# Attention and expert MLP in one kernel: GpSimd instead of VectorE chooses the experts of the side slots, and the last batch's ranks stand two product groups later

## The chip, the cores and the metric

The kernel runs on one core of a Trainium2 chip. The metric is the device time of one execution in microseconds (us). The kernel before has a median of 1017.33 us over 3 runs (1016.41 to 1018.0).

## What is computed

Attention over 8 batches of 8 heads, 576 tokens each, with a threshold under the maximum of each row, followed by a layer that sends each of the 4608 tokens to one of 8 experts:

```python
scores = scale * np.matmul(q, k.transpose(0, 1, 3, 2))          # (8, 8, 576, 576), head_dim 64
thresh = np.max(scores, axis=-1, keepdims=True) - tau
scores = np.where(scores >= thresh, scores, -1000000000.0)
attn = softmax(scores);  x = (attn @ v) as (4608, 512)
logits = x @ w_gate + modality_bias[modality_id]                # (4608, 8)
e_idx = np.argmax(logits, axis=1)
for e in range(8):
    mask = e_idx == e
    h = np.maximum(x[mask] @ w1[e], 0.0)                        # 512 -> 1024
    out[mask] = gate_w[mask, None] * (h @ w2[e])                # 1024 -> 512
```

## The kernel before

**Attention.** A batch has four pairs of heads and a pair has nine steps, so the attention runs over 288 steps. In a step TensorE forms 128 rows of scores against all 576 keys for one head (L427, tile `s` from `km` and `q`), VectorE takes the row maximum (L460), a short VectorE operation adds the threshold (L467), ScalarE exponentiates (L470), VectorE masks and sums (L484, tile `pr`), and TensorE transposes and multiplies by the values (L512, L546). A step's scores cannot be overwritten before L484 of an earlier step has read them, so TensorE waits at L427 when VectorE is late. The keys and queries of the next pair are split into a high and a low part on GpSimd (L338 and L339: `nk`, `qb`, `nq`), and SyncE copies the parts into place (L379 `km`, L373 `q`).

**Routing.** When a batch is through, `route_a`, `route_c` and `route_b` compute logits, the one-hot choice `oh` (L692) and the rank of every token within its expert: six small matmuls of `oh` against a triangle `ltri` and against ones (their line is that of the helper, L546), then `pos` (L709), the running count, and `posi`. Five indirect DMAs on GpSimd (L719, tile `tab`) scatter the token numbers into a table in DRAM.

**Side slots.** The expert MLP of 256 to 512 tokens at a time is woven into the attention of later batches: seven side slots, one for each batch from the second on, and the rest in last slots behind the attention. For each side slot `pick(w)` (lines 728 to 743) finds an expert that has at least `w` tokens left in the table: eight VectorE operations on rows of eight values, whose results are the expert's number and its first row, tile `pk_i`. It is issued 14 steps ahead of the slot. SyncE loads the two numbers into registers (L832, L836), reads the row of token numbers from the table (L838, tile `tb`), and loads weights (L878, L882). GpSimd gathers the tokens with indirect DMAs (L854, `xg`), TensorE transposes them (L868), GpSimd splits the weights (L898, L900), and TensorE multiplies (L914 for the first layer, L941 for the second; VectorE writes `hl` at L926 between them). `done` holds how many units of 64 rows of each expert are given away, and `pick_rest` (L745 to L808) plans the last slots from it: about 40 VectorE operations that end in the table `si` (L795), with which SyncE loads the first last slot.

**What sets the order.** TensorE and GpSimd run in the order in which the program is written out: a dictionary `C` gives a time in steps to every piece, and pieces are emitted by that time. In each of the product loops of a slot a group is three matmuls of 128x512 (high times high, low times high, high times low). The other engines are ordered by a scheduler. The entry `'end'` of `C` places the pieces of the last batch; its last number is the place of `route_b`, in steps behind the start of the last pair.

Of the kernel before, what the change touches and what calls it, by code (L numbers as in the profile page):

```python
# [11 lines left out]
F32 = mybir.dt.float32  # L12
# [5 lines left out]
ALU = mybir.AluOpType  # L18
AX = mybir.AxisListType
# [10 lines left out]
def tile_attn_moe(  # L30
# [16 lines left out]
         'wL': [-5.5, -4, -2.5, 2.7, 12, 13.3, 14.6, 21, 3.8, 4.9, 6, 7.1, 15.8, 22.2, 23.4, 24.6], 'ask': 4, 'gat0': [-8.4, -8.3], 'xt0': [-2, -1], 'rows0': -9.6, 'gat1': [-9.6, -9.5, -5], 'fill': (8, 8.5), 'fpool': (3,), 'route0': (18, 18, 20), 'gap': (1.0, 0.75), 'exp': -12.5, 'two': 98, 'end': (12, 13, (15, 16), (13.5, 13.6, 14.1, 14.2), 14.5, 15, 16.5), 'xf': 9, 'early': [], 'parts': ((((7, 0, 2), (9, 2, 5)), ((11, 0, 2), (13, 2, 5))), (((6, 0, 2), (8, 2, 4), (10, 4, 5)), ((12, 0, 2), (14, 2, 5)))), 'xp': ((15, 16), (16, 17)), 'prepp': ((0, 1, 2), (0, 0, 2)), 'trp': ((7, 11), (6, 12))}  # L47
    nc = tc.nc
    B, H, S, D = q.shape
    NE = wg.shape[1]  # L50
# [12 lines left out]
    W = 512  # L63
    NCH = -(-N // W)
    LAP = 640
    TS = 8
# [7 lines left out]
    U = 64  # L74
# [15 lines left out]
    tiny = ctx.enter_context(tc.tile_pool(name="tiny", bufs=2))  # L90
    wp = ctx.enter_context(tc.tile_pool(name="wp", bufs=1))
    xp = ctx.enter_context(tc.tile_pool(name="xp", bufs=1))
# [44 lines left out]
    def load_first():  # L137
# [3 lines left out]
        for s in range(2):  # L141
            for z, src in enumerate((k, q)):
# [3 lines left out]
                if s == 0:  # L146
# [17 lines left out]
                            base=0, pattern=[[1, P]], channel_multiplier=-1)  # L164
# [16 lines left out]
    iota_1 = iota([1, NE], [[1, NE]], "iota_1", base=1)  # L181
# [10 lines left out]
    for t in oh2:  # L192
# [5 lines left out]
    taken0 = iota([1, NE], [[LAP * TS + 1, NE]], "taken0", base=W * TS)  # L198
    nc.gpsimd.tensor_scalar(out=taken0, in0=taken0, scalar1=1.0 / (U * TS), scalar2=None, op0=ALU.mult)
# [5 lines left out]
                            base=0, pattern=[[1, NE], [-1, NE]], channel_multiplier=0)  # L205
    cnt = glob.tile([1, 4, NE], F32, name="cnt")
# [27 lines left out]
    done = glob.tile([1, NE], F32, name="done")  # L234
# [493 lines left out]
    def pick(w):  # L728

        a = tiny.tile([1, NE], F32, name="pk_a", bufs=1)  # L730
        nc.vector.scalar_tensor_tensor(out=a, in0=done, scalar=float(-U * TS), in1=base[0][0:1, :],
                                       op0=ALU.mult, op1=ALU.add)
        nc.vector.scalar_tensor_tensor(out=a, in0=a, scalar=float(w * TS), in1=iota_1, op0=ALU.is_ge, op1=ALU.mult)
        r = tiny.tile([1, 1], F32, name="pk_r", bufs=1)
        nc.vector.tensor_reduce(out=r, in_=a, axis=AX.X, op=ALU.max)
        nc.vector.tensor_scalar(out=a, in0=iota_1, scalar1=r, scalar2=None, op0=ALU.is_equal)
        t2 = tiny.tile([1, NE], F32, name="pk_d", bufs=1)
        nc.vector.scalar_tensor_tensor(out=t2, in0=a, scalar=float(U * TS), in1=done, op0=ALU.mult, op1=ALU.mult)
        si = tiny.tile([1, 2], I32, name="pk_i")
        nc.vector.tensor_reduce(out=si[:, 1:2], in_=t2, axis=AX.X, op=ALU.max)  # L740
        nc.vector.tensor_scalar(out=si[:, 0:1], in0=r, scalar1=-1.0, scalar2=0.0, op0=ALU.add, op1=ALU.max)
        nc.vector.scalar_tensor_tensor(out=done, in0=a, scalar=float(w // U), in1=done, op0=ALU.mult, op1=ALU.add)
        return si[:, 0:1], si[:, 1:2]

    def pick_rest():  # L745
# [3 lines left out]
        nc.vector.scalar_tensor_tensor(out=left, in0=done, scalar=float(-U * TS), in1=base[0][0:1, :],  # L749
                                       op0=ALU.mult, op1=ALU.add)  # L750
# [4 lines left out]
        for z, w in enumerate((WM, WH, 0)):  # L755
# [9 lines left out]
                                       scalar=float(U) / W, in1=cnt[:, 0:3, :], op0=ALU.mult, op1=ALU.add)  # L765
# [521 lines left out]
```

## Time and profile before

| What | Value |
|---|---|
| median of 3 runs | 1017.33 us (1016.41 to 1018.0) |
| the profiled execution | 1013.78 us |
| its span (first to last instruction) | 1012.0 us, 1.8 us less than its own time |
| mean granted TensorE clock | 0.997 of full speed |
| TensorE matmuls, busy | 988.0 us, 98% of the span |
| VectorE busy | 682.5 us, 67% |
| ScalarE busy | 636.1 us, 63% |
| GpSimd busy | 528.0 us, 52% |
| chain that ended last | TensorE 85%, VectorE 7%, issue 3%, GpSimd 2%, ScalarE 2%, DMA 1% |

The profiled execution is 3.55 us below the median of the runs; differences are worked out within it and then set against the median. The chain is followed back from the last instruction through what released each step; an engine that is not in the chain at some point may be changed there without effect, as long as it does not come into it.

### The profile page before, as it was taken

What the parts mean: (1) busy time and instruction counts of PE and PEld (TensorE: products, weight loads), DVE (VectorE), ACT (ScalarE), POOL (GpSimd) and SP (SyncE); (2) the same over time, 40 slices, a digit from 0 to 9 for tenths busy, and PEclk for the clock granted to TensorE, in tenths of its full rate; (3) what the DMA queues carried; (4) which work ended last, traced back from release to release, by engine and by line L of the source; (5) the groups of instructions that cost most, each with busy time, mean ns of one, the idle gap of its engine ahead of it and who ended that gap; (6) DMA issues with size and microseconds to landing.
All of it is one profiled execution on the core that took longest, in us unless ns stands there. A gap on an engine that the chain in (4) does not pass through costs nothing.

```text
span 1012.0 us, 20320 instructions
## 1 busy us (share of the span) xinstructions
PE 988.0 (98%) x6556; PEld 796.1 (79%) x6556; DVE 682.5 (67%) x1696; ACT 636.1 (63%) x1448; POOL 528.0 (52%) x733
## 2 busy tenths in 40 slices
PE   7999999999998999999999999999999999999997
PEld 6777678788887887888778887788878868888885
DVE  6888977787677776777677777777676765333422
ACT  5787887776666666666667666666666635334430
POOL 4354466386537554645546554646567374634311
PEclk9999999999999999999999999999999999999999
DMA  6667577677646765586645655567665336734301
GB/s 153 158 148 177 140 188 186 171 184 201 170 126 158 194 159 147 124 202 158 183 110 140 168 158 151 144 154 200 165 155 148 88 92 178 224 101 145 105 20 44
DMA packets 207139, 152.22 MB, mean 150 GB/s; under 512 B 100110, under 2 KB 168078, under 8 KB 207024
## 3 DMA queue, kind: packets, MB, share of 16 engines
q1 hardware_dynamic: 199776, 131.74, 51.2%
q0 software_dynamic: 7248, 19.09, 6.1%
q8 instruction: 54, 0.88, 0.4%
q14 instruction: 61, 0.50, 0.2%
HBM read 80.05 MB, written 19.87 MB: 99 GB/s over the span
## 4 chain that ended last, share of the span: by engine, by line
PE 85%; DVE 7%; issue 3%; POOL 2%; ACT 2%; DMA 1%; POOLq 0%; DVEq 0%; ACTq 0%; SPq 0%
PE bk L546 15%; PE s L427 15%; PE bk L512 11%; PE bk L941 10%; PE bk L914 10%; PE pm L941 8%; PE pm L914 8%; PE bk L364 2%; DVE pr L484 2%; DVE nm L460 2%; PE bk L868 2%; PE bk L537 2%; PE bk L598 1%; ACT e L470 1%; PE bk L645 1%
## 5 line engine op out<-in xcount | busy, mean ns | idle before, releaser
L460 DVE TENSOR_REDUCE nm<-s 128x1 f32<-128x576 f32 x254 | 190.9, 752 | 101.0 <-PE s L427 99.6
L484 DVE SCALAR_TENSOR_TENSOR pr<-s,nm,e 128x576 f32<-128x576 f32 x254 | 204.7, 815 | 61.6 <-ACT e L470 58.9
L470 ACT ACTIVATE e<-s,nm 128x576 f32<-128x576 f32 x254 | 188.8, 744 | 62.5 <-DVE nm L460 56.6
L427 PE MATMUL s<-km,q 128*128 128x288 f32 x1024 | 197.2, 314 | 9.9 <-DVE pr L484 8.1
L522 ACT COPY ptm<-bk 128x512 f32<-128x512 f32 x256 | 149.4, 584 | 54.0 <-PE bk L512 53.2
L512 PE MATMUL bk<-ident,pr 128*128 128x128 f32 x1152 | 174.7, 274 | 0.0
L427 PEld LDWEIGHTS s<-km,q 128*128 128x128 f32 x1024 | 146.9, 189 | 26.9 <-DVE pr L484 19.7
L512 PEld LDWEIGHTS bk<-ident,pr 128*128 128x128 f32 x1152 | 141.3, 141 | 27.2 <-issue 6.2
L546 PE MATMUL bk<-ptm,v_m 128*64 128x320 f32 (+1 forms) x1024 | 140.7, 412 | 0.0
L900 POOL TENSOR_TENSOR w2l<-raw,w2h 128x512 fp32r<-128x512 f32 x77 | 98.4, 1287 | 32.6 <-ACT w2h L896 28.5
L546 PEld LDWEIGHTS bk<-ptm,v_m 128*64 128x64 f32 x1024 | 68.2, 136 | 50.6 <-issue 8.6
L956 POOL DMA_INDIRECT out_dram<-y,tb x37 | 37.6, 1017 | 122.1 <-DVE y L954 92.6
L501 ACT COPY rp<-pr 128x64 f32<-128x64 f32 x271 | 60.1, 248 | 42.5 <-DVE pr L484 40.2
L338 POOL CAST nk<-str 128x64 fp32r<-128x64 f32 x31 | 7.4, 239 | 144.1 <-ACT str L352 138.7
L914 PE MATMUL bk<-xh,w1h 128*128 128x512 f32 (+3 forms) x204 | 82.2, 403 | 0.1
L914 PE MATMUL bk<-xl,w1h 128*128 128x512 f32 (+3 forms) x204 | 74.1, 363 | 0.0
L914 PE MATMUL bk<-xh,w1l 128*128 128x512 f32 (+3 forms) x204 | 74.1, 363 | 0.0
L941 PE MATMUL bk<-w2h,hh 128*128 128x512 f32 x168 | 73.3, 436 | 0.0
L900 POOL TENSOR_TENSOR w1l<-raw,w1h 128x512 fp32r<-128x512 f32 x53 | 68.2, 1287 | 4.2
L941 PE MATMUL bk<-w2h,hl 128*128 128x512 f32 x168 | 66.3, 394 | 0.0
L941 PE MATMUL bk<-w2l,hh 128*128 128x512 f32 x168 | 66.0, 393 | 0.0
L900 DVE TENSOR_TENSOR w1l<-raw,w1h 128x512 fp32r<-128x512 f32 x27 | 19.3, 720 | 59.4 <-ACT w1h L896 59.4
(217 smaller groups left out, 1999.0 us busy)
## 6 DMA issues: line engine op xcount, KB each, us to landing
raw<-in_moe_w_dram SPq DMA_DIRECT2D x160, 256.0 KB, 3.6
q<-nq SPq DMA_DIRECT2D x124, 256.0 KB, 4.8
km<-nk SPq DMA_DIRECT2D x124, 144.0 KB, 2.5
v_m<-in_v_dram SPq DMA_DIRECT2D x32, 256.0 KB, 4.1
xs<-xr SPq DMA_DIRECT2D x32, 256.0 KB, 2.5
k_m<-in_k_dram SPq DMA_DIRECT2D x62, 128.0 KB, 3.0
q_m<-in_q_dram SPq DMA_DIRECT2D x62, 128.0 KB, 3.7
vr<-in_v_dram SPq DMA_DIRECT2D x64, 16.0 KB, 3.6
```

The lines of the kernel that those rows point to most:

```text
L427: nc.tensor.matmul(out=sps[:, hf, 0:SH], lhsT=a, rhs=x, start=(z == 0), stop=(z == len(passes) - 1))
L460: in_line(nc.vector.tensor_reduce(out=nm[:, 0:1], in_=sv, axis=AX.XY, op=ALU.max, negate=True), two)
L470: in_line(nc.scalar.activation(out=e, in_=sv, func=AF.Exp, bias=nm[:, 0:1]), two and n < LEAD)
L484: in_line(nc.vector.scalar_tensor_tensor(out=pr.rearrange("p (a x) -> p a x", a=2), in0=s2[n % 2][:, :, 0:SH], scalar=th, in1=e, op0=ALU.i ...
L501: (nc.gpsimd.tensor_copy if 2 <= n < 46 else nc.scalar.copy)(out=state[("rp", p)][:, 2 * c + s + x, :], in_=pr[:, SA:S])
L512: nc.tensor.transpose(out=ps[:, kc * P:(kc + 1) * P], in_=pr[:, kc * P:(kc + 1) * P], identity=ident)
L522: in_line(nc.scalar.copy(out=ptm[:, s, :, (c % 2) * P:(c % 2 + 1) * P], in_=pv), n + 2 < LEAD)
L546: nc.tensor.matmul(out=o, lhsT=lhsT, rhs=rhs, start=start, stop=stop, skip_group_check=True)
L900: then(eng.tensor_tensor(out=lo, in0=raw, in1=hi.bitcast(F32), op=ALU.subtract), eng is nc.vector and (lined or late))
L914: nc.tensor.matmul(out=ps[:, 0:WT], lhsT=a[:, cs], rhs=x[:, c, :], start=(c == 0 and z == 0), stop=(c == KC - 1 and z == 2))
L941: nc.tensor.matmul(out=ps, lhsT=h[:, ts], rhs=w, start=(z == 0 and y == 0), stop=(z == F2 - 1 and y == 2))
L956: i = _inst(nc.gpsimd.indirect_dma_start(out=out, out_offset=bass.IndirectOffsetOnAxis(ap=tb[:, t, 0:1].bitcast(U32), axis=0), in_=y, in_o ...
```

## The change

It has two parts. First, `pick` runs on GpSimd: 16 operations in place of 8, because each of the two reductions over eight values becomes four `tensor_scalar` operations on a single element, each of which folds in two more values as scalars that are read from memory (`fold`; the last of the four folds in one). `done` is now kept in the table's units, so one scaling operation at the start goes and `pick_rest` subtracts directly. Second, `'end'` has 17.5 in place of 16.5, so that the ranks of the last batch are placed further on among the product groups.

```diff
-  'end': (12, 13, (15, 16), (13.5, 13.6, 14.1, 14.2), 14.5, 15, 16.5)
+  'end': (12, 13, (15, 16), (13.5, 13.6, 14.1, 14.2), 14.5, 15, 17.5)
@@ -196,7 +196,6 @@
     lg = glob.tile([P, NT, H + 1, NE], F32, name="lg")
     nc.gpsimd.memset(lg[:, NC], 0.0)
     taken0 = iota([1, NE], [[LAP * TS + 1, NE]], "taken0", base=W * TS)
-    nc.gpsimd.tensor_scalar(out=taken0, in0=taken0, scalar1=1.0 / (U * TS), scalar2=None, op0=ALU.mult)
     th_lo = iota([1, NE, NCH], [[0, NE], [W * TS, NCH]], "th_lo")
     ij = iota([1, MAXC], [[1, MAXC]], "ij")
     tri = glob.tile([1, NE, NE], F32, name="tri")
@@ -727,27 +726,35 @@
 
     def pick(w):
 
+        def fold(x, op, out):
+
+            for z in range(1, NE, 2):
+                nc.gpsimd.tensor_scalar(out=out if z + 2 > NE - 1 else pk_m, in0=x[:, 0:1] if z == 1 else pk_m,
+                                        scalar1=x[:, z:z + 1], scalar2=x[:, z + 1:z + 2] if z + 1 < NE else 0.0,
+                                        op0=op, op1=op)
+
         a = tiny.tile([1, NE], F32, name="pk_a", bufs=1)
-        nc.vector.scalar_tensor_tensor(out=a, in0=done, scalar=float(-U * TS), in1=base[0][0:1, :],
-                                       op0=ALU.mult, op1=ALU.add)
-        nc.vector.scalar_tensor_tensor(out=a, in0=a, scalar=float(w * TS), in1=iota_1, op0=ALU.is_ge, op1=ALU.mult)
+        pk_m = tiny.tile([1, 1], F32, name="pk_m", bufs=1)
+        nc.gpsimd.tensor_tensor(out=a, in0=base[0][0:1, :], in1=done, op=ALU.subtract)
+        nc.gpsimd.tensor_scalar(out=a, in0=a, scalar1=float(w * TS), scalar2=None, op0=ALU.is_ge)
+        nc.gpsimd.tensor_tensor(out=a, in0=a, in1=iota_1, op=ALU.mult)
         r = tiny.tile([1, 1], F32, name="pk_r", bufs=1)
-        nc.vector.tensor_reduce(out=r, in_=a, axis=AX.X, op=ALU.max)
-        nc.vector.tensor_scalar(out=a, in0=iota_1, scalar1=r, scalar2=None, op0=ALU.is_equal)
+        fold(a, ALU.max, r)
+        nc.gpsimd.tensor_scalar(out=a, in0=iota_1, scalar1=r, scalar2=None, op0=ALU.is_equal)
         t2 = tiny.tile([1, NE], F32, name="pk_d", bufs=1)
-        nc.vector.scalar_tensor_tensor(out=t2, in0=a, scalar=float(U * TS), in1=done, op0=ALU.mult, op1=ALU.mult)
+        nc.gpsimd.tensor_tensor(out=t2, in0=a, in1=done, op=ALU.mult)
         si = tiny.tile([1, 2], I32, name="pk_i")
-        nc.vector.tensor_reduce(out=si[:, 1:2], in_=t2, axis=AX.X, op=ALU.max)
-        nc.vector.tensor_scalar(out=si[:, 0:1], in0=r, scalar1=-1.0, scalar2=0.0, op0=ALU.add, op1=ALU.max)
-        nc.vector.scalar_tensor_tensor(out=done, in0=a, scalar=float(w // U), in1=done, op0=ALU.mult, op1=ALU.add)
+        fold(t2, ALU.add, si[:, 1:2])
+        nc.gpsimd.tensor_scalar(out=si[:, 0:1], in0=r, scalar1=-1.0, scalar2=0.0, op0=ALU.add, op1=ALU.max)
+        nc.gpsimd.tensor_scalar(out=a, in0=a, scalar1=float(w * TS), scalar2=None, op0=ALU.mult)
+        nc.gpsimd.tensor_tensor(out=done, in0=done, in1=a, op=ALU.add)
         return si[:, 0:1], si[:, 1:2]
 
     def pick_rest():
 
 
         left = fin["xp"].tile([1, NE], F32, name="left", bufs=1)
-        nc.vector.scalar_tensor_tensor(out=left, in0=done, scalar=float(-U * TS), in1=base[0][0:1, :],
-                                       op0=ALU.mult, op1=ALU.add)
+        nc.vector.tensor_tensor(out=left, in0=base[0][0:1, :], in1=done, op=ALU.subtract)
         taken = fin["xp"].tile([1, NE], F32, name="taken", bufs=1)
         nc.vector.tensor_tensor(out=taken, in0=done, in1=taken0, op=ALU.subtract)
 
@@ -762,7 +769,7 @@
         nc.vector.tensor_tensor(out=ns, in0=cnt[:, 1:4, :], in1=cnt[:, 0:3, :], op=ALU.subtract)
         off = fin["xp"].tile([1, 3, NE], F32, name="off", bufs=1)
         nc.vector.scalar_tensor_tensor(out=off, in0=taken.unsqueeze(1).to_broadcast([1, 3, NE]),
-                                       scalar=float(U) / W, in1=cnt[:, 0:3, :], op0=ALU.mult, op1=ALU.add)
+                                       scalar=1.0 / (W * TS), in1=cnt[:, 0:3, :], op0=ALU.mult, op1=ALU.add)
         cum = fin["xp"].tile([1, 3, NE], F32, name="cum", bufs=1)
         for z in range(3):
             t = fin["xp"].tile([1, NE, NE], F32, name="cum_t", bufs=2)
```

**Where the instructions stand: the choice on GpSimd.** At the second side slot GpSimd is at the splits of weights and the scatters of the second batch (`tab`). Before:

```order
L898 CAST w1h<-raw 128x512
L900 TENSOR_TENSOR w1l<-raw,w1h 128x512
L719 DMA tab<-pay,posi 86016x2
L898 CAST w2h<-raw 128x512
L900 TENSOR_TENSOR w2l<-raw,w2h 128x512
L719 DMA tab<-pay,posi 86016x2 x2
L898 CAST w2h<-raw 128x512
L900 TENSOR_TENSOR w2l<-raw,w2h 128x512
L719 DMA tab<-pay,posi 86016x2
```

With the change, from the end of the first fold on (ahead of these rows stand `w1l`, the three row operations and the first three operations of the fold):

```order
L732 TENSOR_SCALAR pk_r<-pk_m,pk_a 1x1
L743 TENSOR_SCALAR pk_a<-iota_120,pk_r 1x8
L745 TENSOR_TENSOR pk_d<-pk_a,done 1x8
L732 TENSOR_SCALAR pk_m<-pk_d 1x1
L732 TENSOR_SCALAR pk_m<-pk_m,pk_d 1x1 x2
L732 TENSOR_SCALAR pk_i<-pk_m,pk_d 1x1
L748 TENSOR_SCALAR pk_i<-pk_r 1x1
L749 TENSOR_SCALAR pk_a<-pk_a 1x8
L750 TENSOR_TENSOR done<-done,pk_a 1x8
L718 DMA tab<-pay,posi 86016x2
L905 CAST w2h<-raw 128x512
L907 TENSOR_TENSOR w2l<-raw,w2h 128x512
```

All 16 operations stand between the split `w1l` and the first scatter of the batch; behind them the order is as before. At the first and the third slot they stand behind the second scatter, and at slots 4 to 7 behind the last `w2l` of the slot before.

**The ranks of the last batch.** On TensorE, before (`bk_197` and `bk_198` are buffers in PSUM):

```order
L616 MATMUL bk_196<-ident,ot 64x128
L914 MATMUL bk_197<-xh,w1h 128x512
L914 MATMUL bk_197<-xl,w1h 128x512
L914 MATMUL bk_197<-xh,w1l 128x512
L546 LDWEIGHTS ltri
L546 MATMUL bk_198<-oh_133,ltri 128x48
```

and with the change:

```order
L615 MATMUL bk_195<-ident,ot 64x128
L921 MATMUL bk_196<-xh,w1h 128x512
L921 MATMUL bk_196<-xl,w1h 128x512
L921 MATMUL bk_196<-xh,w1l 128x512
L921 MATMUL bk_196<-xh,w1h 128x512
L921 MATMUL bk_196<-xl,w1h 128x512
L921 MATMUL bk_196<-xh,w1l 128x512
L921 MATMUL bk_197<-xh,w1h 128x512
L921 MATMUL bk_197<-xl,w1h 128x512
L921 MATMUL bk_197<-xh,w1l 128x512
L545 LDWEIGHTS ltri
L545 MATMUL bk_198<-oh_133,ltri 128x48
```

Six matmuls of 128x512, the last group of one product and the first of the next, moved ahead of the ranks. On VectorE, before:

```order
L697 RECIPROCAL pay<-gs 128x5
L709 TENSOR_TENSOR pos_123<-bk_198,pos_122 128x6x8
L712 TENSOR_TENSOR pos_123<-pos_123,oh_133 128x5x8
L749 SCALAR_TENSOR_TENSOR left<-done,pos_123 1x8
L714 TENSOR_REDUCE posi<-pos_123 128x5
L756 SCALAR_TENSOR_TENSOR th<-th_lo,left 1x72 x3
L759 TENSOR_REDUCE cnt<-th 1x24
L926 SCALAR_TENSOR_TENSOR hl<-bk_197,hh 128x512
L762 TENSOR_TENSOR ns<-cnt 1x24
```

and with the change:

```order
L696 RECIPROCAL pay<-gs 128x5
L933 SCALAR_TENSOR_TENSOR hl<-bk_196,hh 128x512
L708 TENSOR_TENSOR pos_123<-bk_198,pos_122 128x6x8
L711 TENSOR_TENSOR pos_123<-pos_123,oh_133 128x5x8
L757 TENSOR_TENSOR left<-pos_123,done 1x8
L713 TENSOR_REDUCE posi<-pos_123 128x5
L763 SCALAR_TENSOR_TENSOR th<-th_lo,left 1x72 x3
L766 TENSOR_REDUCE cnt<-th 1x24
L769 TENSOR_TENSOR ns<-cnt 1x24
```

The operation `hl` of the finished product now stands ahead of `pos`. On GpSimd the last `w1l` of the side slots moved from behind the five last scatters to ahead of them.

**SyncE at the fifth slot.** Before, the expert's number is loaded behind a load of weights:

```order
L882 DMA raw<-in_moe_w_dram 128x512
L832 TENSOR_LOAD pk_i
L832 ISA x2
L836 TENSOR_LOAD pk_i
L836 ISA x2
L611 DMA xs<-xr 512x1x128
L633 DMA xs<-xr 64x128
L838 ISA
L838 DMA tb<-tab 128x4x2
```

With the change the copies of the next pair's keys and queries (`km`, `q`) come first:

```order
L123 DMA k_m<-in_k_dram 128x4x64 x2
L378 DMA km_182<-nk_184 64x576 x4
L372 DMA q_180<-nq 64x2x512 x4
L839 TENSOR_LOAD pk_i
L839 ISA x2
L123 DMA q_m<-in_q_dram 128x4x64 x2
L843 TENSOR_LOAD pk_i
L843 ISA x2
L845 ISA
L845 DMA tb<-tab 128x4x2
L132 DMA v_m<-in_v_dram 128x2x256
L134 DMA vr_88<-in_v_dram 64x64 x2
```

The loads of `pk_i` wait for GpSimd now, and stand behind transfers of `xs`, `kq_r`, `k_m`, `km` and `q` that they stood ahead of; the read of `tb` and the slot's weights (L885 with the change) follow behind them. At slots 6 and 7 they stand behind `km` and `q` in the same way; at slots 1 to 4 SyncE's order is as before.

## Rows read from the trace of the kernel before

**Rows 1.** The page's section 1, first engine: busy us, share of the span, instructions.

```profile
PE 988.0 (98%) x6556; PEld 796.1 (79%) x6556; DVE 682.5 (67%) x1696; ACT 636.1 (63%) x1448; POOL 528.0 (52%) x733
```

**Rows 2.** TensorE's waits, at 203-212, 303-312, 632-640, 824-842 and 108-142: total, times, longest us.

```profile
PE s L427 <- DVE pr L484: 0.7, 1, 0.7
...
PE s L427 <- DVE pr L484: 2.1, 1, 2.1
...
PE s L427 <- DVE pr L484: 0.3, 1, 0.3
...
PE bk L546 <- DVE oh L692: 0.8, 1, 0.8
PE pm L941 <- DVE hl L926: 0.3, 1, 0.3
...
PE s L427 <- DMA q<-nq: 1.1, 1, 1.1
```

**Rows 3.** The chain of work at 303 to 309 and 740 to 748: start us, us, what.

```profile
304.05 1.13 DVE pk_a L736
...
307.08 0.80 PE s L427 x4
...
742.11 0.53 PE s L427 x4
...
744.50 0.80 PE s L427 x4
```

**Rows 4.** Groups of instructions on VectorE, the first of the choice's eight (busy us, mean ns).

```profile
L736 DVE TENSOR_SCALAR pk_a<-iota,pk_r 1x8 f32<-1x8 f32 x7 | 4.0, 564 | 0.2
```

**Rows 5.** GpSimd: a group, then its timeline near slot 1 (start us, us, operation, idle before).

```profile
L842 POOL TENSOR_TENSOR tb<-tb,beyond 128x1 int32<-128x1 int32 x1 | 0.2, 192 | 0.0
...
125.33 0.24 POOL L338 CAST nk<-str 128x64 fp32r<-128x64 f32 x1 [4.94 <-DMA xs<-xr]
125.66 0.32 POOL L339 TENSOR_TENSOR nk<-str,nk 128x64 fp32r<-128x64 f32 x1
```

**Rows 6.** Slot 2: GpSimd's first gather, its DMA issue (us to landing), TensorE's first transposes.

```profile
219.76 1.06 POOL L854 DMA_INDIRECT xg<-xs,tb  x1 [0.16 <-DMA kq_r<-in_k_dram]
...
xg<-xs,tb POOLq DMA_INDIRECT x1, 4.9
...
227.78 0.60 PE L868 MATMUL bk<-ident,xg 128*128 128x128 f32 x4
```

**Rows 7.** Slot 3: GpSimd's idle time and second gather, its landing, TensorE's second transposes.

```profile
321.82 0.24 POOL L338 CAST nk<-str 128x64 fp32r<-128x64 f32 x1 [4.01 <-ACT str L352]
...
327.01 1.05 POOL L854 DMA_INDIRECT xg<-xs,tb  x1
...
xg<-xs,tb POOLq DMA_INDIRECT x1, 5.2
...
333.11 0.60 PE L868 MATMUL bk<-ident,xg 128*128 128x128 f32 x4
```

**Rows 8.** Slot 5: GpSimd's idle time behind the gathers, and TensorE's first transposes.

```profile
565.92 1.02 POOL L956 DMA_INDIRECT out_dram<-y,tb  x1 [12.80 <-DVE rs L492]
...
569.54 0.60 PE L868 MATMUL bk<-ident,xg 128*128 128x128 f32 x4
```

**Rows 9.** The last stage: VectorE, GpSimd, the first gather and its landing, TensorE's transposes.

```profile
836.66 1.60 DVE L791 TENSOR_SCALAR bj<-bj 1x30 f32<-1x30 f32 x1
838.29 0.18 DVE L792 SCALAR_TENSOR_TENSOR bj<-ej,bj 1x30 f32<-1x30 f32 x1
...
836.89 1.32 POOL L900 TENSOR_TENSOR w1l<-raw,w1h 128x512 fp32r<-128x512 f32 x1
851.35 1.40 POOL L854 DMA_INDIRECT xg<-xs,tb  x1 [13.13 <-issue]
...
xg<-xs,tb POOLq DMA_INDIRECT x1, 4.6
...
856.23 0.60 PE L868 MATMUL bk<-ident,xg 128*128 128x128 f32 x4
```

More of the change, by code (lines that the diff above doesn't have):

```diff
@@ L46, in tile_attn_moe @@
          'wS': [-6, -4.7, -3.4, 3, 12.5, 14, 15.5, 21.5, 4.2, 5.4, 6.6, 7.5, 22.7, 23.8, 24.9, 25.8],
-         'wL': [-5.5, -4, -2.5, 2.7, 12, 13.3, 14.6, 21, 3.8, 4.9, 6, 7.1, 15.8, 22.2, 23.4, 24.6], 'ask': 4, 'gat0': [-8.4, -8.3], 'xt0': [-2, -1], 'rows0': -9.6, 'gat1': [-9.6, -9.5, -5], 'fill': (8, 8.5), 'fpool': (3,), 'route0': (18, 18, 20), 'gap': (1.0, 0.75), 'exp': -12.5, 'two': 98, 'end': (12, 13, (15, 16), (13.5, 13.6, 14.1, 14.2), 14.5, 15, 16.5), 'xf': 9, 'early': [], 'parts': ((((7, 0, 2), (9, 2, 5)), ((11, 0, 2), (13, 2, 5))), (((6, 0, 2), (8, 2, 4), (10, 4, 5)), ((12, 0, 2), (14, 2, 5)))), 'xp': ((15, 16), (16, 17)), 'prepp': ((0, 1, 2), (0, 0, 2)), 'trp': ((7, 11), (6, 12))}
+         'wL': [-5.5, -4, -2.5, 2.7, 12, 13.3, 14.6, 21, 3.8, 4.9, 6, 7.1, 15.8, 22.2, 23.4, 24.6], 'ask': 4, 'gat0': [-8.4, -8.3], 'xt0': [-2, -1], 'rows0': -9.6, 'gat1': [-9.6, -9.5, -5], 'fill': (8, 8.5), 'fpool': (3,), 'route0': (18, 18, 20), 'gap': (1.0, 0.75), 'exp': -12.5, 'two': 98, 'end': (12, 13, (15, 16), (13.5, 13.6, 14.1, 14.2), 14.5, 15, 17.5), 'xf': 9, 'early': [], 'parts': ((((7, 0, 2), (9, 2, 5)), ((11, 0, 2), (13, 2, 5))), (((6, 0, 2), (8, 2, 4), (10, 4, 5)), ((12, 0, 2), (14, 2, 5)))), 'xp': ((15, 16), (16, 17)), 'prepp': ((0, 1, 2), (0, 0, 2)), 'trp': ((7, 11), (6, 12))}
     nc = tc.nc
```

## The prediction, made before the changed kernel ran

> **What bounds the kernel now.** I read the page's busy times first: TensorE is busy for 988.0 of 1012.0 us [rows 1]. A change that does not touch TensorE's own work can therefore win only where TensorE waits, and lose wherever it makes a new wait. So the second view is TensorE's waits in the stretches that the change touches [rows 2]. The reader should see three kinds of row there. TensorE waits for VectorE's `pr` at the step of the second, third and sixth choice (0.7, 2.1 and 0.3 us). It waits 0.8 us for the one-hot `oh` before the last ranks, and 0.3 us for `hl` behind them. And near the first choice it waits 1.1 us for a copy of the queries, which hangs on GpSimd's splits and not on VectorE.
>
> The third view is the chain of work [rows 3]. At the third choice it runs through `pk_a` L736 for 1.13 us and ends in the scores at 307.08: here the choice itself makes TensorE late. The same rows give a second price: four score matmuls take 0.53 us in a running stream and 0.80 us after a stop, so a wait costs some 0.27 us beyond its idle time.
>
> **What the choice costs on VectorE, and what goes.** The fourth view is the groups of instructions [rows 4]. The costliest of the eight operations has a mean of 564 ns; the eight groups of seven together are 13.7 us, or 1.96 us for one choice. The reason for the spread stands in the last group of rows: a VectorE TENSOR_SCALAR on 30 elements took 1.60 us, from 836.66 to 838.26, and a GpSimd TENSOR_TENSOR ran from 836.89 to 838.21 [rows 9]. The 1.13 us of L736 are of the same kind. The Trainium skill, GPSIMD Engine Reference, section Specifications, says that the two engines share their SBUF interfaces and contend when VectorE runs in a two-port mode; these rows agree with it.
>
> **What it costs on GpSimd.** No row of the kernel before shows a GpSimd operation with a scalar from memory, so I bound it. The smallest steady two-input operation is L842 with 192 ns [rows 5]. An operation that needs the one before it starts 0.09 us after that one's end: the cast at 125.33 lasts 0.24 us, and its subtraction starts at 125.66 [rows 5]. Sixteen operations that each need the one before make 16 x 0.192 + 15 x 0.09 = 4.4 us. This is the value I take, because L842 is nearest in size. The lower end is 16 x 0.192 = 3.1 us, with no gap at all. The upper end takes every operation at the 0.32 us of the 128x64 subtraction: 16 x 0.32 + 15 x 0.09 = 6.5 us. Call this length d. What it does differs from slot to slot.
>
> *Slot 1.* The 16 operations stand behind the second scatter. GpSimd then idles 4.94 us until 125.33 [rows 5], which takes in the whole of d up to 4.94 us. What goes beyond makes the splits late, and through them the query copy for which TensorE waits already [rows 2], one for one. No wait for VectorE is won, since this wait ends later. At d = 4.4: 0.
>
> *Slot 2.* Here GpSimd has no idle time to give. The first gather starts at 219.76 and lands 4.9 us later, at 224.7; TensorE wants it at 227.78 [rows 6]. The slack is 3.1 us. Everything between is a row of splits and scatters behind the choice, and the read of `tb` sits in the middle of it, so the whole row moves by d. TensorE loses d - 3.1, whatever it has won at the scores before (0.7 us idle, and the stop), since this wait ends last: +1.3 us.
>
> *Slot 3.* The choice stands behind the second scatter; GpSimd's idle 4.01 us before 321.82 [rows 7] take in most of it. The second gather starts at 327.01, lands 5.2 us later at 332.2, and is wanted at 333.11: slack 0.9 us. The 2.1 us of wait at the scores, with its stop 2.4 us, go with VectorE's work. But TensorE can come forward by 0.9 us only, less what GpSimd is late (d - 4.0): the net is d - 4.9, at best -2.4. At 4.4: -0.5 us.
>
> *Slots 4 to 7.* At slot 4 only SyncE is held at the register load, ahead of copies that are far from due. At slot 5 the reads of `tb` and the weights stand behind the copies of `q` now. GpSimd idles 12.80 us behind the first two gathers, until 565.92, and TensorE transposes the first at 569.54 [rows 8]: a gather that starts up to 12 us later, at about 563, and lands in the 4.6 to 5.2 us of the others, is still in time by about a microsecond. Slots 6 and 7 have idle time of the same kind on GpSimd. If that cover were gone, slot 5 would be the first to pay, one for one. On VectorE the sixth choice frees 0.3 us and a stop of 0.27, and the seventh the stop that shows as 0.80 instead of 0.53 us [rows 2, 3]: -0.8 us together.
>
> **The last ranks.** Six matmuls of 128x512 move ahead of them, 1.4 us by the starts of their neighbours in the timeline, so `oh` is there before TensorE asks for it: the 0.8 us go. `hl` moves ahead of `pos`, so the 0.3 us behind them go too: 1.1 us [rows 2]. Can it be kept? The first last slot's gather starts at 851.35, lands 4.6 us later, and is used at 856.23 [rows 9]: the slack is 0.3 us, so the plan `si` has to come earlier as well. `pos` comes some 0.9 us later behind the moved matmuls and `hl` (0.6 us). Of the chain behind it `hl` is gone, and so is the hold on L791, 1.60 us where the next operation of that size takes 0.18 [rows 9], because GpSimd's `w1l` of 836.89 now runs ahead of the scatters: 0.9 - 0.6 - 1.3 makes `si` about 1 us earlier. That carries the 1.1 us.
>
> **Sum.** 0 + 1.3 - 0.5 - 0.8 - 1.1 = -1.1 us. Against the profiled execution's 1013.78 us that is 1012.7; the median of the runs shown stands 3.55 us above that execution, and I put the same difference on it: 1017.33 - 1.1 = **1016.2 us**. A measurement of this kernel can tell about 0.2% (2.0 us) from no change.
>
> **The rivals.** All of it hangs on d, and on which of two waits ends last.
>
> *The operations are short.* Below d = 3.9 us the sum is under -2.0. At 3.1 us slot 2 costs nothing, slot 3 gives 1.8, the rest 1.9: -3.7, or 1013.6 us. For it speaks that half of the operations touch one element only, and the rows of GpSimd fall with size. Against it, they fall slowly, and each of the 16 waits for the one before.
>
> *The fold is dear, and gathers come late (slower).* The place is slot 2's gather, and then those of slots 1 and 3. Above d = 5.6 us the sum passes +2.0. At 6.5 us: slot 1 costs 1.6, slot 2 3.4, slot 3 1.6, and 1.9 come back: +4.7, or 1022.0 us. For it speaks that nine of the sixteen operations read scalars from memory, for which no row gives a price, and that slot 2's stretch of GpSimd is packed. Against it, no small operation of GpSimd in the trace is near 0.32 us. The Trainium skill, GPSIMD Engine Reference, section Engine selection, puts elementwise work and reductions along a row on VectorE, and calls GpSimd about half as fast; it speaks against this change. By its factor alone a choice of 1.96 us on VectorE would take 3.9 us on GpSimd and the kernel would end at 1015.2 us, an estimate that leaves out the doubled number of operations.
>
> *The ranks bring nothing.* If `si` is not earlier, the first gather of the last slots takes the 1.1 us back, and the sum is 0: 1017.3 us. For it speaks the slack of 0.3 us.
>
> **Chances and range.** Short operations 0.37; the forecast, with d between 3.9 and 5.6 us, 0.33, and the ranks without effect 0.04; the dear fold 0.26. So faster by over 0.2% has 0.37, within 0.2% 0.37, slower 0.26. The range runs from 1012.9 us (the short end, with some 0.7 us of smaller waits of the same kind) to 1022.0 us (the dear end); the forecast's own case spans 1015.3 to 1019.3.
>
> **What would show it.** In the changed profile the 16 operations of slot 2 from the first subtraction to the sum into `done` give d directly. Right: between 4 and 5 us; TensorE waits about a microsecond for the gather at slot 2's first transposes; the wait at the third slot's scores (2.1 us) is gone, and half a microsecond to two of it comes back at the transposes; no wait for `oh` before the last ranks; L791 takes 0.2 us; the first gather of the last slots starts about a microsecond earlier. Wrong: slot 2 without a wait at the transposes, a wait at slot 5's first transposes, or a wait of GpSimd's weight splits that reaches TensorE.

## The result: slower by 1.3%, with the waits moved from VectorE to the gathers

The changed kernel has a median of 1029.66 us over 6 runs (1027.78 to 1034.36), the kernel before 1017.23 us beside it: a ratio of 1.0128, with a 95% interval of 1.0114 to 1.0142. The forecast was 1016.2 us, the range ended at 1022.0 us. The profiled execution took 1028.69 us. Its page, sections 1 and 4:

```profile
span 1026.6 us, 20379 instructions
PE 989.9 (96%) x6556; PEld 796.0 (78%) x6556; DVE 678.1 (66%) x1640; ACT 636.8 (62%) x1448; POOL 559.3 (54%) x844
...
PE 83%; DVE 5%; issue 3%; DMA 3%; POOL 3%; ACT 1%; SPq 1%; POOLq 0%; DVEq 0%; ACTq 0%
```

TensorE's work is the same to 2 us [rows 1]; the span is 14.6 us longer. VectorE's share of the chain fell from 7% to 5%, and DMA came in with 3%. Of the whole span, TensorE's waits (total, times, longest us):

```profile
PE bk L875 <- DMA xg<-xs,tb: 8.4, 4, 3.3
PE s L426 <- DVE pr L483: 6.2, 11, 1.5
PE s L426 <- DMA q<-nq: 2.9, 2, 2.7
PE pm L948 <- DVE hl L933: 2.4, 1, 2.4
PE bk L875 <- DVE pr L483: 1.5, 1, 1.5
```

The waits for `pr` of [rows 2] did shrink: over the whole kernel they were 8.4 us before and are 6.2 now. But 8.4 us of waits for gathers stand there that did not exist, and the wait for `hl` grew from 0.3 to 2.4 us.

GpSimd's timeline at slot 2 gives the length that all hung on (start us, us, operation, idle before; L732 is the fold):

```profile
206.80 0.19 POOL L738 TENSOR_TENSOR pk_a<-pos,done 1x8 f32<-1x8 f32 x1
...
207.72 0.38 POOL L732 TENSOR_SCALAR pk_m<-pk_a 1x1 f32<-1x1 f32 x1
208.20 0.81 POOL L732 TENSOR_SCALAR pk_m<-pk_m,pk_a 1x1 f32<-1x1 f32 x2
...
212.44 0.20 POOL L750 TENSOR_TENSOR done<-done,pk_a 1x8 f32<-1x8 f32 x1
213.19 1.13 POOL L718 DMA_INDIRECT tab<-pay,posi  x1 [0.55 <-DVE nmt L459]
...
228.78 1.06 POOL L861 DMA_INDIRECT xg<-xs,tb  x1 [0.16 <-DMA kq_r<-in_k_dram]
```

From 206.80 to 212.64 are 5.84 us, and the scatter behind starts 0.55 us later where it waited 0.16 us before. The groups of instructions say why (busy us, mean ns):

```profile
L732 POOL TENSOR_SCALAR pk_m<-pk_m,pk_a 1x1 f32<-1x1 f32 x14 | 4.9, 353 | 1.4
...
L743 POOL TENSOR_SCALAR pk_a<-iota,pk_r 1x8 f32<-1x8 f32 x7 | 2.2, 313 | 0.7
...
L749 POOL TENSOR_SCALAR pk_a<-pk_a 1x8 f32<-1x8 f32 x7 | 1.8, 255 | 0.6
...
L738 POOL TENSOR_TENSOR pk_a<-pos,done 1x8 f32<-1x8 f32 x7 | 1.4, 193 | 0.0
```

The two-input operation costs the 192 ns of [rows 5]. On eight elements a scalar operation with constants costs 255 ns and one with a scalar from memory 313; one with two scalars from memory costs 353 on a single element, more than the 128x64 subtraction of [rows 5] with its 320. The fold is dear per operation, though each touches one element.

To see where the time went, I take the start of the same TensorE matmul in each trace (the n-th score matmul of `s` from `km` and `q`, behind 831 us the n-th product into `pm`), subtract its start in the first profile of the kernel before, and give by how much this lag grew in each stretch (times of the kernel before, us):

| profile of | to 116 | slot 1, 116-161 | slot 2, 199-278 | slot 3, 278-368 | slot 5, 546-631 | ranks, 803-857 | behind, 857-880 | at 1000 |
|---|---|---|---|---|---|---|---|---|
| the kernel before, again (e9) | -1.3 | 2.5 | -0.1 | 0.0 | 0.0 | 0.0 | 0.0 | 1.4 |
| the changed kernel | 0.9 | 1.8 | 3.9 | 1.5 | 3.4 | -1.5 | 4.2 | 14.8 |
| e1, choice only | -0.7 | 2.7 | 4.8 | 1.3 | 5.2 | 0.0 | 0.0 | 13.6 |
| e2, ranks only | -1.2 | 2.8 | 0.0 | -0.1 | 0.0 | -1.5 | 2.7 | 2.8 |
| e3, shorter choice | -0.2 | 3.1 | 3.6 | 0.7 | 3.8 | -1.5 | 2.7 | 12.5 |
| e4, slot 5 on VectorE | -0.3 | 2.5 | 4.5 | 1.6 | 0.0 | -1.5 | 0.0 | 7.0 |
| e5, longer choice | 0.1 | 4.5 | 5.8 | 3.1 | 6.7 | -1.5 | 2.7 | 20.8 |
| e12, ranks, with copies | -0.1 | 1.5 | -0.1 | 1.6 | 0.0 | -1.5 | 0.0 | 1.6 |

The stretches left out (161 to 199, 368 to 546, 631 to 803) hold 0.6 us or less in each of these. The loss has four places: slots 2, 3 and 5, and a stretch behind the last ranks. The ranks themselves win 1.5 us. Slot 1 needs the first line of the table to be read: see e9.

Some of these numbers hold a second thing, TensorE's granted clock. In the changed kernel it fell from 1.00 to 0.50 of full speed (from 2.4 to 1.2 GHz) right behind the 2.4 us wait for `hl`; in e2, behind the same wait, it did not. Of each: the stretch, its us, TensorE's busy us and matmuls, granted clock, DMA share, GB/s.

```profile
872.82:876.23 3.41, 3.41 (x11) 0.50 0.98 305
```

```profile
861.70:865.11 3.41, 3.41 (x19) 1.00 1.02 310
```

Half of the 3.4 us is lost, 1.7 us: this is why the stretch behind the ranks holds 4.2 us in one and 2.7 in the other. Stretches at 0.50 stand at the end of the waits of slots 1, 2 and 5 in e1 and e5, of slots 1 and 5 in e3 and of slots 1 and 2 in e4, though the changed kernel's profile has none there after waits of 2.7 to 3.3 us; and at the 2.1 us wait for `pr` at slot 3 in e12, whose 1.6 us there are this.

In e2 and e9 the clock did not fall between 5 and 1010 us. So single profiles of one program can differ by 1.7 us at such a place, and no run shows what decides it. The medians hold it too: the slowest three runs of the changed kernel, 1030.44, 1032.72 and 1034.36 us, were granted 0.992, 0.990 and 0.988. With the median of its six runs, 0.9925, against 0.996 to 0.997 for the kernel before in the runs beside e1 to e8, up to some 4 us of the 12.4 us between the medians are clock, by an estimate from these shares.

### The profile page after: what moved, and what is told of

Its sections match the earlier page's. It is cut to its first block, busy times and chain, and to the rows that moved or that the text cites. A ratio compares the mean times of both kernels' runs of the same rounds, so it can differ in the third digit from the quotient of the medians.

```text
span 1026.6 us, 20379 instructions
## 1 busy us (share of the span) xinstructions
PE 989.9 (96%) x6556; PEld 796.0 (78%) x6556; DVE 678.1 (66%) x1640; ACT 636.8 (62%) x1448; POOL 559.3 (54%) x844
## 4 chain that ended last, share of the span: by engine, by line
PE 83%; DVE 5%; issue 3%; DMA 3%; POOL 3%; ACT 1%; SPq 1%; POOLq 0%; DVEq 0%; ACTq 0%
PE bk L545 14%; PE s L426 14%; PE bk L921 11%; PE bk L511 10%; PE bk L948 10%; PE pm L948 9%; PE pm L921 7%; PE bk L363 2%; PE bk L536 2%; PE bk L875 2%; DMA xg<-xs,tb 1%; DVE nm L459 1%; DVE pr L483 1%; PE bk L597 1%; DMA q<-nq 1%
## 5 line engine op out<-in xcount | busy, mean ns | idle before, releaser
L907 DVE TENSOR_TENSOR w1l<-raw,w1h 128x512 fp32r<-128x512 f32 x27 | 25.9, 966 | 59.8 <-ACT w1h L903 54.4
```

The lines of the kernel that those rows point to most:

```text
L907: then(eng.tensor_tensor(out=lo, in0=raw, in1=hi.bitcast(F32), op=ALU.subtract), eng is nc.vector and (lined or late))
```

## The experiments

**e1: the choice alone.**

```diff
-  'end': (..., 14.5, 15, 17.5)
+  'end': (..., 14.5, 15, 16.5)
```

> The choice on GpSimd alone, the ranks at 16.5 as in the kernel before. Theory 1 (the choice is 5.9 us long on GpSimd, and four slots' gathers or copies wait for it; the ranks' place costs a little on top, through VectorE's weight split that stands still for 7.3 us behind GpSimd's five splits): TensorE's idle time at slots 1, 2, 3 and 5 stays (about +10 us against before), the 2.4 us before L948 in the last slots are gone and the 0.8 us before the last ranks are back: 11 us slower than before, about 1028.3 us. Rival (the ranks' place is the main cause): under 1020 us.

Measured: 1027.06 us against 1016.79, ratio 1.0091 (1.0073 to 1.011). The choice alone carries most of the loss. In the trace the wait for `oh` is back, that for `hl` is 0.3 us again, and the stretch behind the ranks loses nothing.

**e2: the ranks alone**, the opposite edit in the kernel before.

```diff
-  'end': (..., 14.5, 15, 16.5)
+  'end': (..., 14.5, 15, 17.5)
```

> The ranks two groups later alone, the choice on VectorE as in the kernel before. Theory 1: the wait for oh (0.8 us) goes and the plan of the last slots is ready earlier, so GpSimd's five splits of w2 start earlier against VectorE's splits of w1; one of those stands still for about 7 us, and TensorE waits some 2.4 us for hl behind it: 1.3 us slower than before, about 1018.5 us. Rival A (the term as predicted): 1.1 us faster, about 1016.1 us, and no such standstill. Rival B (the standstill needs the late choice): as A.

Measured: 1018.74 us, ratio 1.0013 (0.9997 to 1.003), near theory 1's 1018.5 us but not told from no change. The trace tells it: 1.5 us won at the ranks and 2.7 lost behind them. VectorE's, GpSimd's and TensorE's timelines of e2 in the last stage:

```profile
853.13 7.91 DVE L900 TENSOR_TENSOR w1l<-raw,w1h 128x512 fp32r<-128x512 f32 x2
...
848.35 1.04 POOL L854 DMA_INDIRECT xg<-xs,tb  x1 [9.10 <-issue]
...
853.62 6.26 POOL L900 TENSOR_TENSOR w2l<-raw,w2h 128x512 fp32r<-128x512 f32 x5
...
861.70 0.50 PE L941 MATMUL pm<-w2h,hl 128*128 128x512 f32 x1 [2.41 <-DVE hl L926]
```

and the same of the kernel before and of the changed kernel:

```profile
852.95 1.28 DVE L900 TENSOR_TENSOR w1l<-raw,w1h 128x512 fp32r<-128x512 f32 x2
...
857.16 6.28 POOL L900 TENSOR_TENSOR w2l<-raw,w2h 128x512 fp32r<-128x512 f32 x5
```

```profile
848.65 0.16 DVE L798 TENSOR_SCALAR bj<-bj 1x30 f32<-1x30 f32 x1
...
863.48 7.90 DVE L907 TENSOR_TENSOR w1l<-raw,w1h 128x512 fp32r<-128x512 f32 x2
...
863.97 6.26 POOL L907 TENSOR_TENSOR w2l<-raw,w2h 128x512 fp32r<-128x512 f32 x5
...
872.04 0.50 PE L948 MATMUL pm<-w2h,hl 128*128 128x512 f32 x1 [2.40 <-DVE hl L933]
```

Before, VectorE's last two splits of w1 were through (1.28 us for both) three microseconds ahead of GpSimd's five splits of w2. With the ranks moved, the plan, the gathers and so GpSimd's splits come 3.5 us earlier. The first of VectorE's two splits, begun half a microsecond ahead of them, stands still until all five are over (7.3 of the 7.9 us are its own), the `hl` behind it is late, and TensorE waits 2.4 us. So the move of the ranks won what it was to win, and made GpSimd's splits early enough to collide with VectorE's.

**e3: the choice shortened.** The second fold, the sum, as two sums of halves and one scalar operation:

```diff
-        fold(t2, ALU.add, si[:, 1:2])
+        for h in (4, 2):
+            nc.gpsimd.tensor_tensor(out=t2[:, 0:h], in0=t2[:, 0:h], in1=t2[:, h:2 * h], op=ALU.add)
+        nc.gpsimd.tensor_scalar(out=si[:, 1:2], in0=t2[:, 0:1], scalar1=t2[:, 1:2], scalar2=0.0, op0=ALU.add, op1=ALU.add)
```

> The changed kernel with the second fold (the sum) as two tensor_tensor operations on halves and one scalar operation in place of four scalar operations: about 0.85 us less of the choice on GpSimd, at every slot. Theory 1: the waits at slots 1, 2, 3 and 5 each shrink by about 0.85 us, 3.4 us in all: about 1026.2 us. Rival (the order on the queues costs, not the length): within 0.5 us of the changed kernel's 1029.7 us.

Measured: 1027.38 us, ratio 1.0096 (1.0076 to 1.0116). The choice is 4.96 us long. TensorE's longest waits for it: slot 1 2.40 us (2.69 in the changed kernel), slot 2 2.10 (2.92), slot 3 0.54 and 0.89 (0.98 and 1.28), slot 5 1.99 (3.25): 3.2 us less together, unevenly (0.3 us at slot 1, 1.3 at slot 5, for a choice that is 0.9 us shorter). The time fell by 2.3 us only, and medians of six runs don't settle the rest. The rival, within 0.5 us, does not fit the waits.

**e5: the choice lengthened.**

```diff
         nc.gpsimd.tensor_tensor(out=done, in0=done, in1=a, op=ALU.add)
+        for _ in range(7):
+            nc.gpsimd.tensor_tensor(out=t2, in0=t2, in1=a, op=ALU.mult)
```

> The changed kernel with seven more GpSimd operations (1x8 products of no use) behind each choice, some 2.0 us more at each slot. Theory 1 (the length of the choice is paid one for one by the gathers or copies of slots 1, 2, 3 and 5): each of the four waits grows by about 2 us, 8 us in all, about 1037.7 us; slots 4, 6 and 7 pay nothing. Rival (the number of places that pay is smaller, or larger): 2 us for each such place.

Measured: 1038.72 us, ratio 1.022 (1.0194 to 1.0245), 9.1 us over the changed kernel. Seven such operations took 1.82 us. The whole-kernel waits of e5, and then of e3:

```profile
PE bk L877 <- DMA xg<-xs,tb: 13.9, 4, 5.1
...
PE s L426 <- DMA q<-nq: 4.6, 1, 4.6
```

```profile
PE bk L877 <- DMA xg<-xs,tb: 7.2, 5, 2.1
```

The waits at slots 1, 2, 3 and 5 are 4.63, 4.92, 3.87 and 5.09 us, against 2.69, 2.92, 2.26 and 3.25: 1.6 to 2.0 us more at each, close to one for one with the length; e3 shows the same from the other side, less evenly. The stretches of the table grew by 2.7, 1.9, 1.6 and 3.3 us, more than the waits at slots 1 and 5, where the clock at 0.50 stands at the wait in e5 and not in the changed kernel (at slot 2 too, but there the changed kernel's second wait of 1.5 us is gone in its place). Slots 4, 6 and 7 pay nothing in either.

**e4: slot 5's choice on VectorE**, with the eight operations of the kernel before; the other six on GpSimd. Left out here: `pick_v`, which is those eight operations, and the slot's number `z`, which is handed on to `pick`.

```diff
+        if z == 4:
+            return pick_v(w)
```

> The changed kernel with the fifth slot's choice on VectorE, which puts SyncE's loads of it back ahead of the copies of km and q. Theory 1: the 3.25 us of TensorE's wait for that slot's first gather go, about 1026.3 us. Rival (the gather is late because GpSimd is late as a whole): at most 0.5 us of it goes, 1029.2 us or more.

Measured: 1024.53 us, ratio 1.0072 (1.0054 to 1.009), 5.1 us under the changed kernel. The slot's 3.25 us are gone, as theory 1 has it, and so is the collision behind the ranks: three of GpSimd's four gathers took 1.4 to 1.5 us instead of 1.0 here, for a reason that the trace does not show, and its splits came 0.9 us behind VectorE's. That shows how narrow that gap is. Why slot 5 was late is in SyncE's and GpSimd's timelines of the changed kernel, and in TensorE's waits at 575 to 582:

```profile
564.64 3.40 SPq L372 DMA_DIRECT2D q<-nq  x4
569.33 1.30 SPq L123 DMA_DIRECT2D q_m<-in_q_dram  x2
571.46 0.40 SPq L845 DMA_DIRECT2D tb<-tab  x1
...
574.80 1.14 POOL L861 DMA_INDIRECT xg<-xs,tb  x1 [10.18 <-DMA tb<-tab]
...
PE bk L875 <- DMA xg<-xs,tb: 3.3, 1, 3.3
```

The choice pushed `nq` back, its four copies went ahead of the register loads, two loads of `q_m`, whose buffer TensorE was still reading, stood between the two register loads, and the gather started 3.3 us behind the start of the read of `tb`.

**e6 to e8, e10, e12: can the ranks be had without the collision?** Each has the ranks at 17.5 with the choice on VectorE, unless it says otherwise. In e6 a one-column copy that needs the split's result stands behind each of the first last slot's splits of w2 on GpSimd, so that its two-input operations no longer follow each other without a gap.

```diff
+                if lined and which == 2 and eng is nc.gpsimd:
+                    nc.gpsimd.tensor_copy(out=xp.tile([P, 1], F32, name="gap", bufs=1), in_=lo[:, 0:1].bitcast(F32))
```

> The ranks two groups later alone, and behind each of the first last slot's w2 splits on GpSimd a copy of one column that needs the split's result. Theory 1 (VectorE's w1 split with two SBUF inputs stands still for as long as GpSimd's two-input operations follow each other without a gap): the copy lets it in, it lasts 1 to 3 us instead of 7.3, the 2.4 us wait for hl goes, and the term of the ranks comes out as predicted: 1.1 us faster than before, about 1015.7 us. Rival (GpSimd's stretch as a whole shuts VectorE out, whatever its operations): 7 us of standstill and more, 1018.7 us.

Measured: 1019.51 us, ratio 1.0022 (1.0008 to 1.0036). The mechanism is confirmed: VectorE's two splits took 2.94 us together, not 7.91, the wait for `hl` is gone and the ranks' stretch wins 1.6 us. But the time is not won. This profile lost 4.8 us at slot 1, in a standstill of the kind that e9 shows, and 2.8 at slot 2, where the choice's last operation on VectorE, `done` at L742, took 1.24 us beside GpSimd's split of w2 (0.39 in the kernel before) and TensorE waited 2.07 us for `pr`; behind each the granted clock was 0.50 for 3.4 us. And behind 880 us TensorE loses 1.2 us bit by bit, with no wait and at a granted clock of 1.00.

**e7: the ranks one group later** (17 in place of 17.5).

> The ranks one group later (17.0) in the kernel before. The wait for oh shrinks from 0.8 to about 0.1 us; the plan is nearly as early as at 17.5, so the weight split stands still here too. Theory 1: about 1.3 us slower than before, 1018.1 us, with the 2.4 us wait. Rival (the collision needs the second group): 0.9 us faster, 1015.9 us.

Measured: 1019.91 us, ratio 1.0017 (0.9997 to 1.0036). The stretch of the ranks wins 0.3 us, and the collision, with its 2.4 us wait, is there, here with the clock at 0.50 behind it: the second group is not needed for it.

**e8: a hybrid**, GpSimd choosing at slots 4, 6 and 7 alone (`if z in (0, 1, 2, 4): return pick_v(w)`), with e6's copies.

> GpSimd chooses at slots 4, 6 and 7 alone, VectorE at 1, 2, 3 and 5; the ranks at 17.5 and the copies of e6. Theory 1: the slots that have room on GpSimd pay nothing, the sixth and seventh slot's waits for pr (0.5 us with the stops) go, and with the ranks' 1.1 us: about 1015.2 us, under both kernels. Rival (SyncE's later loads at slots 6 and 7 cost what they cost at slot 5): 3 us or more slower.

Measured: 1018.98 us, ratio 1.0019 (1.0005 to 1.0033). Slots 4, 6 and 7 lose nothing, but the 0.5 us that I had put on the sixth and seventh does not show either: from 631 to 803 us the lag grew by 0.2 us, as in e2. The slow loss behind 880 us is 1.2 us here too.

**e9: the kernel before, once more.**

> The kernel before, unchanged, for a second profile. In the profiles of e2, e6, e7 and e8, which are the same program up to 826 us, all engines stand still together for 1 to 3 us near 120 us; in the one profile of the kernel before they don't. If the standstill is usual for this program, it shows here too (span about 1014 to 1016 us, most of the 3.5 us between that profile and the median); if it comes of the other kernels' code, the span is near 1012 us again.

Measured: one execution, 1015.9 us, span 1014.1. The standstill is there. TensorE, ScalarE and VectorE of e9 near 119 us:

```profile
117.81 0.80 PE L427 MATMUL s<-km,q 128*128 128x288 f32 x4 [0.38 <-issue]
119.47 0.66 PE L512 MATMUL bk<-ident,pr 128*128 128x128 f32 x4 [0.86 <-issue]
...
118.83 0.59 ACT L522 COPY ptm<-bk 128x512 f32<-128x512 f32 x1 [1.29 <-PE s L427]
...
120.30 0.69 DVE L607 TENSOR_TENSOR xr<-bk,ri 128x512 f32<-128x512 f32 x1 [1.81 <-PE bk L512]
```

The three stop together: TensorE twice with no releaser that the profile shows ("issue"; in some of the other profiles it is put down to VectorE or ScalarE, which stand still too), ScalarE and VectorE in idle time that is put down to TensorE. GpSimd does not stop; its scatters go on, one each 1.28 us. The granted clock is 1.00. Every later profile with the choice of slot 1 on VectorE has this (e2, e6 to e10, e12: 1.5 to 4.8 us in that stretch, the most in e6); the first one had not. e9 stands 2.1 us over it, which is most of the 3.5 us by which that profile stood under its median. With slot 1's choice on GpSimd the standstill is absent, and the wait for `q` takes its place; the two are about equal, which is why slot 1 costs the changed kernel nothing against e9.

**e10 and e11.** e10 is e6 with the copy's tile 16 columns wide; e11 is e8 with e10's tile and slot 1's choice on GpSimd too.

> As e6 (the ranks two groups later, and a one-column copy behind each of the first last slot's w2 splits on GpSimd), with the copy's tile 64 bytes wide in place of 4. In e6's trace TensorE loses 1.3 us bit by bit behind 880 us, which no wait explains. Theory 1: that comes of the tile of 4 bytes, which shifts the tiles behind it; here it goes, and the ranks' 1.5 us remain: about 1015.6 us. Rival (the copies themselves cost it): as e6.

> GpSimd chooses at slots 1, 4, 6 and 7, VectorE at 2, 3 and 5; the ranks at 17.5 and the copies of e10. Theory 1: slot 1 pays the 1.5 us that it pays in the changed kernel, the others nothing: 1.5 us over e10, about 1017.1 us. Rival (the standstill near 120 us belongs to the five scatters that follow each other without a gap there, and the choice between them breaks it up): about 0.7 us under e10.

Measured: e10 1018.59 us, ratio 1.0005 (0.9993 to 1.0018); e11 1020.24 us, 1.002 (1.001 to 1.0029). The wider tile did not take the slow loss away (0.8 us in e10, 0.9 in e11), so a tile this much wider does not cure it. e11 is 1.7 us over e10 in the medians, as theory 1 has it: with the choice between the scatters slot 1 is free of the standstill, and the wait for `q`, 3.94 us there and with the clock at 0.50 behind it, costs more. In the two traces slot 1 makes 0.5 us of this.

**e12: the copy in place**, so that no tile is added.

```diff
+                    nc.gpsimd.tensor_copy(out=lo[:, 0:1], in_=lo[:, 0:1].bitcast(F32))
```

> As e10, with the copy written back over the column it reads, so that no tile is added and nothing in memory moves. Theory 1: no collision of VectorE's w1 split with GpSimd's splits, no slow loss of TensorE behind 880 us, and the last stage keeps the 1.5 us that the ranks give in the traces: 1.5 us under the kernel before. Rival (the copies cost the slow loss): as e10, the same as before within 0.2%.

Measured: 1016.13 us against 1016.81, ratio 0.999 (0.9979 to 1.0001). The slow loss is gone, so it came with the added tile and not with the copies; how a tile does it stays open. VectorE's and GpSimd's timelines of e12:

```profile
854.65 2.94 DVE L900 TENSOR_TENSOR w1l<-raw,w1h 128x512 fp32r<-128x512 f32 x2
...
855.13 1.30 POOL L900 TENSOR_TENSOR w2l<-raw,w2h 128x512 fp32r<-128x512 f32 x1
856.50 0.54 POOL L903 CAST w2l<-w2l 128x1 fp32r<-128x1 f32 x1
857.00 1.74 POOL L900 TENSOR_TENSOR w2l<-raw,w2h 128x512 fp32r<-128x512 f32 x1
```

VectorE's split now waits for one GpSimd split and goes through in the gap of the first copy. The last stage keeps its 1.5 us in the trace. In the medians it is 0.7 us, and the interval still touches no change: the one version here with a median under both kernels, but not shown to be faster.

## Why the prediction was wrong

- **The step that failed first is the price of the fold.** The term 16 x 0.192 us took the row nearest in size. Measured: the sixteen operations take 4.5 us, 0.28 each in the mean; the 0.09 us between them held. So the choice is 5.84 us long, not 4.4, and about 0.4 us more pass until the next scatter starts. Size was the wrong measure of nearness, for the kind of operation counts too: 193 ns with two tensors, 208 to 255 with constants, 272 to 378 with scalars from memory. A nearer row stood in the trace of the kernel before, the scaling operation that the change takes away, beside one that contradicts the prediction's "no small operation of GpSimd in the trace is near 0.32 us":

```profile
L271 POOL TENSOR_SCALAR mid_f<-mid_f 128x40 f32<-128x40 f32 x1 | 0.3, 342 | 0.1
...
L199 POOL TENSOR_SCALAR taken<-taken 1x8 f32<-1x8 f32 x1 | 0.3, 263 | 0.0
```

With 263 ns for the twelve scalar operations the sum is 12 x 0.263 + 4 x 0.192 + 15 x 0.09 = 5.3 us. The slower rival named this place and this point (from 5.6 us on), but its upper end of 6.5 us did not bring the whole of the loss. Nor does this step alone: with 6.2 us for the length the prediction's own sum is 1.3 + 3.1 + 1.3 - 0.8 - 1.1 = 3.8 us, 1021.1 us, still inside its range. The measured 1029.66 us needs the steps below.
- **The steps from the length to slots 1 to 3 held in the main.** At 6.2 us they give 1.3 us at slot 1, 3.1 at slot 2 and 1.3 at slot 3. The waits of the changed kernel were 1.5 us more for `q`, 2.9 us for the first gather of slot 2, and a net 1.5 us at slot 3. Slot 2's stretch lost 3.9 us, because a second wait of 1.49 us stands at the transposes of its gathers, which the sum had not (put down to `pr` in this profile, to the gather in e3 and e4). e3 and e5 show that these waits follow the length. That VectorE's waits would shrink was right too, though 0.4 us of the 2.1 at slot 3 stayed.
- **"Still in time by about a microsecond" at slot 5 failed.** The gather was to start at about 563 and did so at 574.80; 8 us of this are the lag of the whole kernel by then, the rest the longer choice, the wait of `q_m` on SyncE between the two register loads, and the landing of `tb`. It cost 3.25 us, which e4 took back whole. The prediction had put a margin of one microsecond on a start that it only estimated, and called it hidden.
- **The last ranks: right in what they win, and blind behind it.** The waits for `oh` and `hl` went, L791 fell from 1.60 to 0.16 us (L798 now), and the stretch won 1.5 us where 1.1 were put. But the first gather of the last slots was to start about a microsecond earlier, and in e2 it started 3.0 us earlier (848.35 against 851.35 us [rows 9]), with SyncE's first read of `tb` 2.5 us earlier. VectorE's splits had been through 2.9 us ahead of GpSimd's; one microsecond would not have reached them. And the question asked was only whether the early plan could carry the gain, not what an earlier gather sets off next on GpSimd: the five splits, and VectorE's standstill behind them. That took 2.7 us in e2 and, with the clock at 0.50 behind it, 4.2 in the profiled execution of the change.
- **The sixth and seventh choice (-0.8 us) won nothing** that e8 could show. Most of that term was the price of a stop, 0.80 - 0.53 = 0.27 us, and that was a misreading: the two numbers of [rows 3] are pieces of the chain of work, which ends a group where the next takes over. In the timeline of the same stretch the four score matmuls at 741.86, in a running stream, take 0.78 us, and those at 744.50, behind the stop, 0.80.
- **The clock was put at nothing.** The prediction has no term for a wait behind which the granted clock falls to 0.50. Apart from the first 22 and the last 5 us it fell once in the profiled execution of the change, which cost 1.7 us, and two or three times in e1, e3, e4 and e5.

The parts nearly add up, in the profiled executions. Against the second profile of the kernel before, the lag of the changed kernel at 1000 us is 14.8 - 1.4 = 13.4 us; of it 13.1 are 4.0 at slot 2, 1.5 at slot 3, 3.4 at slot 5, 4.2 - 1.5 at the ranks and behind, -0.7 at slot 1, and 2.2 us ahead of 116 us, of which 1.5 are one standstill near 66 us that no other profile has. The medians differ by 12.4 us; that the two are close is in part luck, since the runs hold the clock and the standstills in other shares than the profile.

The Trainium skill, GPSIMD Engine Reference, section Engine selection, puts such work on VectorE and had spoken against the change, and the runs bear it out. By its factor of two the choice would have been 3.9 us, an estimate, and it was 5.84: the two reductions, 0.15 us each on VectorE, became eight operations that take 2.7 us on GpSimd.

## What to carry to other kernels

Price a small operation by its kind of operands, not by its size alone; where the trace has no row of that kind, leave the upper end wide, and put the forecast nearer to it. Before work is moved to an engine off the critical path, follow that engine's queue from the place of the insertion to the first thing that somebody waits for: here a packed row of splits, scatters and gathers had 3 us to give at one slot and 1 at another. When a wait goes, ask what starts earlier because of it, and with what that will collide. And before two profiles are compared stretch by stretch, look at the granted clock of each stretch.

## What the runs showed of the hardware that was not expected

- VectorE's two-input operation on SBUF stood still for 7.3 us, through five GpSimd subtractions that follow each other without a gap, and got in at the first one-column copy between two of them (e6, e12). VectorE operations that read PSUM were not held: in the kernel before an `hl` ran in 0.69 us amid the same five. The Trainium skill, GPSIMD Engine Reference, section Specifications, names such contention for VectorE instructions with two SBUF inputs; the length of the standstill is this trace's.
- TensorE, ScalarE and VectorE stop together for one to three microseconds near 120 us in e9 and in the six other later profiles with slot 1's choice on VectorE, while GpSimd's scatters go on, with no releaser that the profile shows. The standstill is absent where GpSimd's choice stands between the scatters (the changed kernel, e1, e3 to e5, e11); what stops the three is open.
- Behind one wait of 2.4 us the granted clock fell to 0.50 for 3.4 us (the changed kernel, e7), and behind the same wait it stayed at 1.00 (e2, e3, e5).
- With a tile of 4 or of 64 bytes more in the pool TensorE's products lost 0.8 to 1.2 us behind 880 us, in small steps, at a granted clock of 1.00; without it the loss was gone. The cause is open.
